# Taking the sign of float64 weights from GpSimd to ScalarE in a fused attention and bilinear MoE kernel

## The chip, the cores and the metric

The kernel runs on one core of one Trainium2 chip. The metric is the device time of one execution in microseconds; the figure compared is the median over several runs. The core has TensorE (PE in the profile), VectorE (DVE), ScalarE (ACT), GpSimd (POOL) and SyncE (SP), which here only issues DMAs.

## What is computed

The reference joins a pooled attention to a bilinear mixture layer. `q`, `k`, `v` have the shape (4, 8, 1152, 64); the weights come as float64 arrays.

```python
q_pool = q.reshape(B, H, S // 2, 2, D).mean(axis=3)          # 576 rows a head
scores = (1 / sqrt(D)) * q_pool @ k.T                         # 576 x 1152 a head
attn = exp(scores - max); attn = attn / (attn.sum() + 1e-9)
x = (attn @ v)  ->  (2304 tokens, 512)
out = ((x @ w_a) * (x @ w_b)) @ w_out                          # 512 -> 1536 -> 512
```

## The kernel before, in words

Work is cut into tasks. Each task is one small function of the kernel (`w_load`, `w_tail`, `w_sign`, `sm_max`, `moe_mm` and so on), registered by `add` with an engine, a planned cost and the names of the buffers that it reads and writes. `Plan.order` takes for each engine the sequence written out by hand in the table `ORDERS` (one list of task numbers for each of PE, DVE, ACT, POOL and SP) and merges the five lists; every engine then runs its own list strictly in order, and waits by semaphores where a buffer of another engine is not ready.

**Attention.** The 16 pairs of heads go by in passes; the first batch (pairs 0 to 3) goes in two rounds, the rest in one. A pass has blocks of 128 rows: TensorE makes the scores (`qk`, L768 or, split into halves of 16 bits, L770), VectorE reads them with a running minimum (`sm_max`, L800), ScalarE takes the exponential (`sm_exp`, L807), VectorE adds a constant and inverts the sum (`sm_sum` L811, `sm_rec` L817). From the second round on, ScalarE then writes the upper half of the probabilities in 16 bits (`sm_hi`, L820) and VectorE the rest (`sm_lo`, L824) into one of NPB buffers `p`; a DMA on the SP queue transposes the buffer into `pt` (L829), and TensorE multiplies by `v` (`pv`, L918). A buffer `p` may be written again when its transposition has landed. The four passes of the first round transpose on TensorE instead (L842) and use no `p`.

**Weights.** Behind the first four passes 36 tiles of 128 x 512 weights are prepared: f = 0 to 11 of `w_a`, `w_b` (m = 0, 1) and `w_out` (m = 2). A float64 arrives as two words of 32 bits in one of NRAW = 7 buffers `raw` (numbers 5 and 6 of them lie in `xt`). For each tile VectorE takes the largest magnitude of the upper words (`w_mag`, L596; then the short `w_real`, L602 and L604, `w_scale`, L646 and L650); ScalarE reduces the lower word to three bits (`w_tail`, L614); GpSimd reads the upper word as float32 and writes its sign as a 16-bit zero with a sign into the top of the lower word (`w_sign`, L618); ScalarE rescales the upper word in place (`w_z`, L609); VectorE shifts it left by three and joins the lower word to it by an OR (`w_join`, L624). The shift drops the sign bit of the upper word, so the sign comes from the lower word. Then ScalarE and GpSimd, or VectorE for `w_out`, split the float32 into two halves of 16 bits (`w_hi` L707, `w_lo` L712 or L714). The joined tile of `w_out` number f stands in the place of number f + 1 in `wo`, and one spare place at the end serves number 11.

**Bilinear layer.** Nine tiles of 256 tokens each run `moe_mm` (L999, TensorE), `moe_a` (L1034, ScalarE), `moe_g` (L1037, VectorE), the split `moe_gh` and `moe_gl` (L1042, L1045) and `moe_o` (L1064, TensorE), between the blocks of later passes; the last three tiles run after the last scores.

Of the kernel before, what the change touches and what calls it, by code (L numbers as in the profile page):

```python
# [92 lines left out]
    ),  # L93
    (
# [231 lines left out]
def kernel(  # L326
# [13 lines left out]
    def T(name, shape, dtype=F32):  # L340
        return sb.tile(shape, dtype, name=name)

    NS, NPB, NST, NG, NR = 3, 3, 12, 2, 6
    NRAW, NT_ = 7, 2 * B + 1
    wab = T("wab", [128, NF, 2, 2, KC, 128], F16)
    wo = T("wo", [128, NF + 1, 2, DM], F16)
# [56 lines left out]
    def ri(n):  # L403
        return n % NRAW
# [911 lines left out]
```

## Time and profile before

| | us |
|---|---|
| median of 3 runs | 824.94 |
| lowest and highest | 824.78, 828.25 |
| the profiled execution, its own time | 827.88 |
| span in its profile | 826.1 |
| TensorE busy in the span | 758.5 (92%) |
| VectorE busy | 647.6 (78%) |
| ScalarE busy | 570.8 (69%) |
| GpSimd busy | 228.8 (28%) |

Busy is time in which an engine works on an instruction, so an instruction that is held up in the middle counts as busy for its whole length. The shares are means over the whole span, and the load is not the same in all its stretches: it has to be looked at by stretches. A wait in the views stands for an engine that was idle, with the work that ended the idle time.

### The profile page before, as it was taken

How to read it: one execution, taken by the hardware profiler on the slowest of the kernel's cores; microseconds unless marked ns; L12 is line 12 of the kernel's file. 1: busy time of each engine (PE TensorE's matmuls, PEld its weight loads, DVE VectorE, ACT ScalarE, POOL GpSimd, SP SyncE). 2: the span in 40 equal slices, each digit the busy share in tenths (PEclk: the TensorE clock that was granted, in tenths of full speed). 3: DMA queues.
4: the chain of work that ended last, by engine and by line, in shares of the span. 5: the costliest groups of instructions: out<-in, count | busy, mean ns of one | idle time of the engine just before them, and what ended most of it. 6: DMA issues, size and time to landing. Idle time of an engine off the chain costs nothing. (4 is left out here: it accounts for less than half of the span.)

```text
span 826.1 us, 21393 instructions
## 1 busy us (share of the span) xinstructions
PE 758.5 (92%) x8906; PEld 564.5 (68%) x8906; DVE 647.6 (78%) x1283; ACT 570.8 (69%) x940; POOL 228.8 (28%) x206
## 2 busy tenths in 40 slices
PE   7787589988899988899999987999999999999998
PEld 5665367754677755687588645886687578677775
DVE  5989989999988888879979899898888984222222
ACT  5989879989777778768876887678767974321211
POOL 3879767943201122010402041103020320000000
PEclk9999689999999999999999999999999999999999
DMA  8275588999999999869979999879898976100100
GB/s 331 79 259 182 169 189 232 243 215 162 211 194 203 188 211 181 190 139 191 197 157 212 154 203 206 147 145 185 174 184 160 153 135 114 30 27 1 26 2 26
DMA packets 316433, 132.32 MB, mean 160 GB/s; under 512 B 300848, under 2 KB 302896, under 8 KB 316336
## 3 DMA queue, kind: packets, MB, share of 16 engines
q1 hardware_dynamic: 316336, 130.96, 76.0%
q8 instruction: 69, 1.13, 0.6%
q14 instruction: 28, 0.23, 0.1%
HBM read 50.72 MB, written 4.72 MB: 67 GB/s over the span
## 5 line engine op out<-in xcount | busy, mean ns | idle before, releaser
L999 PEld LDWEIGHTS <-wab 128*128 128x128 f16 x2592 | 251.3, 98 | 40.9 <-issue 4.5
L999 PE MATMUL ab<-xt,wab 128*128 128x256 f16 x2304 | 262.6, 273 | 3.6 <-DVE g L1037 2.4
L807 ACT ACTIVATE s<-s,st 128x1152 f32<-128x1152 f32 x144 | 179.7, 1248 | 23.3 <-DVE s L800 22.1
L824 DVE SCALAR_TENSOR_TENSOR p<-s,st,p 128x1152 f16<-128x1152 f32 x128 | 183.3, 1436 | 13.4 <-ACT p L820 12.5
L820 ACT ACTIVATE p<-s,st 128x1152 f16<-128x1152 f32 x128 | 159.5, 1249 | 48.3 <-DMA pt<-p 18.7
L1045 POOL TENSOR_TENSOR gl<-g,gh 128x256 f16<-128x256 f32 x72 | 60.1, 844 | 311.5 <-ACT gh L1042 195.8
L918 PE MATMUL xps<-pt,vs 128*64 128x128 f16 (+1 forms) x3888 | 109.1, 215 | 5.9 <-DMA pt<-p 3.4
L1037 DVE SCALAR_TENSOR_TENSOR g<-ab,cc,g 128x256 f32<-128x256 f32 x108 | 51.4, 479 | 80.5 <-ACT g L1034 79.8
L918 PEld LDWEIGHTS <-vs 128*64 128x64 f16 x3888 | 100.5, 111 | 18.6 <-issue 14.1
L1034 ACT ACTIVATE g<-ab 128x256 f32<-128x256 f32 x108 | 40.3, 376 | 101.4 <-PE ab L999 101.3
L800 DVE TENSOR_SCALAR_CACHE_REDUCE s<-sps,ksc 128x1152 f32<-128x1152 f32 x72 | 101.0, 1410 | 8.1 <-PE sps L770 7.5
L800 DVE TENSOR_SCALAR_CACHE_REDUCE s<-sps 128x1152 f32<-128x1152 f32 x72 | 96.3, 1349 | 13.2 <-PE sps L768 12.3
L768 PE MATMUL sps<-k,q 64*128 64x512 f32 (+2 forms) x480 | 93.8, 524 | 10.7 <-DVE s L800 9.4
L1064 PE MATMUL ab<-wo,gh 128*128 128x512 f16 x336 | 100.7, 380 | 2.4 <-DVE g L1037 1.0
L768 PEld LDWEIGHTS sps<-k,q 64*128 64x128 f32 (+1 forms) x480 | 61.2, 184 | 43.3 <-issue 21.2
L770 PE MATMUL sps<-k,q 64*128 64x512 f16 (+2 forms) x720 | 65.9, 324 | 6.8 <-DVE s L800 6.5
L1042 ACT ACTIVATE gh<-g 128x256 f16<-128x256 f32 x108 | 43.5, 407 | 38.4 <-PE ab L1064 20.0
L618 POOL TENSOR_SCALAR raw<-raw 128x512 f16<-128x512 f32 x26 | 62.0, 2385 | 22.9 <-ACT raw L614 8.4
L1064 PE MATMUL ab<-wo,gl 128*128 128x512 f16 x168 | 63.7, 379 | 3.8 <-POOL gl L1045 3.8
L1064 PEld LDWEIGHTS <-gh 128*128 128x128 f16 x432 | 39.0, 99 | 41.3 <-ACT gh L1042 1.5
L770 PEld LDWEIGHTS <-q 64*128 64x128 f16 (+1 forms) x720 | 40.3, 96 | 34.9 <-issue 15.2
L1064 PEld LDWEIGHTS <-gl 128*128 128x128 f16 x216 | 21.1, 98 | 33.1 <-POOL gl L1045 8.3
(135 smaller groups left out, 814.6 us busy)
## 6 DMA issues: line engine op xcount, KB each, us to landing
k<-in_k_dram SPq DMA_DIRECT2D x18, 576.0 KB, 5.2
vraw<-in_v_dram SPq DMA_DIRECT2D x17, 576.0 KB, 4.6
raw<-in_w_ab_dram SPq DMA_DIRECT2D x18, 512.0 KB, 4.7
qraw<-in_q_dram SPq DMA_DIRECT2D x12, 576.0 KB, 4.8
raw<-in_w_out_dram SPq DMA_DIRECT2D x8, 512.0 KB, 4.5
out_dram<-o SPq DMA_DIRECT2D x16, 256.0 KB, 2.6
xt<-in_w_ab_dram SPq DMA_DIRECT2D x6, 512.0 KB, 5.6
pt<-p SPq DMA_TRANSPOSE x128, 5.3
```

Source lines behind the costliest of these rows:

```text
L618: nc.gpsimd.tensor_scalar(out=raw_h[ri(n)], in0=raw_t[ri(n)][:, :, 1].bitcast(F32), scalar1=2.0 ** -100, scalar2=None, op0=ALU.mult)
L768: return nc.tensor.matmul(out, q, k, start=True, stop=True)
L770: return nc.tensor.matmul(out, q[:, hq], k[:, hk], start=(hq, hk) == (0, 0), stop=(hq, hk) == (1, 0))
L800: nc.vector.tensor_scalar(out=s_t[sbuf(i)], in0=sps[:, at:at + S], scalar1=-1.0 / 16.0 if u is None else ksc[:, u, 4:5], scalar2=None, op0 ...
L807: nc.scalar.activation(out=s, in_=s, func=AF.Exp, scale=-1.0, bias=t[:, 0:1], accum_out=t[:, 1:2])
L820: nc.scalar.activation(out=p_t[pbuf(i)][:, 0], in_=s_t[sbuf(i)], func=AF.Copy, scale=st_t[i % NST][:, 3:4])
L824: nc.vector.scalar_tensor_tensor(out=p[:, 1], in0=s, scalar=st_t[i % NST][:, 3:4], in1=p[:, 0], op0=ALU.mult, op1=ALU.subtract)
L918: nc.tensor.matmul(xps[half(e), at:at + w], vs[:, c, e, hv], pt[t][:, hp, c, c0:c0 + w], start=(c == 0 and n == 0), stop=(c == NCH - 1 and ...
L999: nc.tensor.matmul(dst if t < 8 else dst.rearrange("p (b n) -> p b n", b=B), wab[:, f, 1 - m, a, c], moe_x(t, b, c), start=(n == 0), stop= ...
L1037: nc.vector.scalar_tensor_tensor(out=g_t[:, f], in0=ab[j][:, 0], scalar=cc[:, t, f:f + 1], in1=g_t[:, f], op0=ALU.mult, op1=ALU.mult)
L1045: (nc.vector if dve else nc.gpsimd).tensor_tensor(out=gl_t[j], in0=g_t[:, f], in1=gh_t[j], op=ALU.subtract)
L1064: nc.tensor.matmul(out_bank(t, u), g[:, us], wo[:, f, a], start=(first and n == 0), stop=(last and n == 2))
```

## The change

`w_sign` goes. `w_z` becomes a parametric ReLU in place of a plain copy: for a negative weight the slope of -2^32 gives the magnitude times 2^32, and so sets a bit of the exponent that the later shift by three moves into the sign bit. One more buffer `p` is there (NPB from 3 to 4). `wo` loses its spare place; the last tile of `w_out` is joined in its `raw` buffer. Some planned costs are altered, and the order table is new: without `w_sign` every task keeps its engine, but tasks are renumbered and stand in another order (matched by name, 446 of 590 places in the list of TensorE hold another task than before, 879 of 1001 on VectorE, 670 of 762 on ScalarE, 165 of 241 on SP). On SP the loads begin q, k, k, w(1,0), w(1,1), v(1), w(2,0), v(0), q(1), k(1), where before they begin q, k, k, w(0,0), w(2,0), w(1,0), w(0,1), q(1), k(1).

```diff
 ORDERS = (
...
-    NS, NPB, NST, NG, NR = 3, 3, 12, 2, 6
+    NS, NPB, NST, NG, NR = 3, 4, 12, 2, 6
...
-    wo = T("wo", [128, NF + 1, 2, DM], F16)
+    wo = T("wo", [128, NF, 2, DM], F16)
...
-    raw_h = [x.rearrange("p n w -> p (n w)").bitcast(F16).rearrange("p (n h) -> p n h", h=4)[:, :, 1] for x in raw_t]
...
+    def in_place(f, m):
+        return m < 2 or f == NF - 1
+
     def zname(f, m):
-        return f"raw{ri(wn(f, m))}a" if m < 2 else f"w{f + 1}2"
+        return f"raw{ri(wn(f, m))}a" if in_place(f, m) else f"w{f + 1}2"
...
     def w_z(f, m, n):
         by = wz[:, 1, m, f:f + 1].bitcast(F32) if m < 2 else 2.0 ** -112
         up = raw_t[ri(n)][:, :, 1].bitcast(F32)
-        nc.scalar.activation(out=up, in_=up, func=AF.Copy, scale=by)
+        nc.scalar.activation(out=up, in_=up, func=AF.Prelu, scale=by, alpha=-(2.0 ** 32))
...
-    def w_sign(n):
-
-        nc.gpsimd.tensor_scalar(
-            out=raw_h[ri(n)], in0=raw_t[ri(n)][:, :, 1].bitcast(F32), scalar1=2.0 ** -100, scalar2=None,
-            op0=ALU.mult
-        )
...
         add("ACT", 0.555, key, w_tail, (n,), w=[rw + "l"])
-        add("POOL", 2.42, key, w_sign, (n,), r=[rw + "a"], w=[rw + "l"], port=False)
...
-        add("ACT", 0.6, key, w_z, (f, m, n), r=[f"wz{f}"] * (m < 2), w=[rw + "a"])
+        add("ACT", 0.65 if m < 2 else 0.56, key, w_z, (f, m, n), r=[f"wz{f}"] * (m < 2), w=[rw + "a"])
...
-        add("DVE", 0.32, key - 5, w_real, (0, 2, f, f + 1), r=mx, w=[x + "r" for x in mx], port=True)
+        add("DVE", 0.27, key - 5, w_real, (0, 2, f, f + 1), r=mx, w=[x + "r" for x in mx], port=True)
...
-        add("POOL", 0.04 * len(which) + 1.18 * n, key, x_lo, (p, j, which), r=xs + [x + "h" for x in names],
+        add("POOL", 0.33 + 0.3 * len(which), key, x_lo, (p, j, which), r=xs + [x + "h" for x in names],
```

## Rows read from the trace of the kernel before

**Rows 1.** The page, first part: span, then busy time by engine.

```profile
span 826.1 us, 21393 instructions
PE 758.5 (92%) x8906; PEld 564.5 (68%) x8906; DVE 647.6 (78%) x1283; ACT 570.8 (69%) x940; POOL 228.8 (28%) x206
```

**Rows 2.** Busy time by stretch: length, engines, TensorE clock, DMA share, GB/s.

```profile
0.00:20.65 20.65, 15.45 (x74) 10.69 (x76) 10.97 (x25) 10.74 (x18) 6.69 (x10) 1.00 0.90 331
20.65:206.50 185.85, 151.68 (x1591) 113.54 (x1587) 175.20 (x376) 164.10 (x291) 132.65 (x84) 0.94 0.75 192
206.50:702.00 495.50, 471.53 (x6236) 353.51 (x6237) 430.73 (x807) 368.09 (x562) 88.47 (x110) 1.00 0.94 176
702.00:826.10 124.10, 119.81 (x1011) 86.71 (x1008) 30.67 (x79) 27.83 (x71) 1.03 (x2) 1.00 0.07 19
```

**Rows 3.** The same view, one slice of the second stretch.

```profile
82.60:103.30 20.70, 10.65 (x68) 8.19 (x70) 20.36 (x43) 17.85 (x28) 15.15 (x11) 0.68 0.54 169
```

**Rows 4.** Groups of VectorE, 20.65 to 206.5 us: busy us, mean ns, idle before.

```profile
L824 DVE SCALAR_TENSOR_TENSOR p<-s,st,p 128x1152 f16<-128x1152 f32 x19 | 27.9, 1482 | 1.1 <-ACT p L820 1.1
L624 DVE SCALAR_TENSOR_TENSOR raw<-raw 128x512 int32<-128x512 int32 x18 | 14.6, 815 | 0.0
...
L714 DVE SCALAR_TENSOR_TENSOR wo<-wo,wr 128x512 f16<-128x512 f32 x11 | 9.4, 856 | 0.1
...
L602 DVE TENSOR_SCALAR wmx<-wmx 128x2 f32<-128x2 f32 (+1 forms) x11 | 5.7, 521 | 0.1
...
L604 DVE TENSOR_SCALAR wmx<-wmx 128x2 int32<-128x2 int32 (+1 forms) x11 | 4.7, 428 | 0.4
...
L650 DVE TENSOR_SCALAR wz<-wz 128x2 int32<-128x2 int32 x12 | 4.2, 354 | 0.4
```

**Rows 5.** Single lines of VectorE, 0 to 206.5 us: shortest, median, longest ns.

```profile
L602 DVE TENSOR_SCALAR wmx<-wmx x13: 151/284/1353, 15.2 to 167.5; 128x2 f32<-128x2 f32 x12, 128x12 f32<-128x12 f32 x1
L604 DVE TENSOR_SCALAR wmx<-wmx x13: 169/170/1306, 16.6 to 167.8; 128x2 int32<-128x2 int32 x12, 128x12 int32<-128x12 int32 x1
L650 DVE TENSOR_SCALAR wz<-wz x12: 169/237/974, 23.8 to 107.4; 128x2 int32<-128x2 int32 x12
L624 DVE SCALAR_TENSOR_TENSOR raw<-raw x18: 667/686/1621, 28.0 to 126.8; 128x512 int32<-128x512 int32 x18
L824 DVE SCALAR_TENSOR_TENSOR p<-s,st,p x19: 1398/1412/1816, 88.8 to 204.1; 128x1152 f16<-128x1152 f32 x19
L714 DVE SCALAR_TENSOR_TENSOR wo<-wo,wr x11: 727/743/1165, 173.7 to 203.4; 128x512 f16<-128x512 f32 x11
```

**Rows 6.** Instructions in order of time, 20 to 62 us: start, length.

```profile
20.85 6.96 POOL L618 TENSOR_SCALAR raw<-raw 128x512 f16<-128x512 f32 x3 [4.34 <-DMA xt<-in_w_ab_dram]
...
26.50 1.34 DVE L602 TENSOR_SCALAR wmx<-wmx 128x2 f32<-128x2 f32 x1
```

**Rows 7.** Groups of GpSimd, 20.65 to 206.5 us.

```profile
L618 POOL TENSOR_SCALAR raw<-raw 128x512 f16<-128x512 f32 x24 | 57.5, 2394 | 16.7 <-PE sps L768 7.7 <-DMA xt<-in_w_ab_dram 4.3 <-ACT raw L614 2.4
L618 POOL TENSOR_SCALAR xt<-xt 128x512 f16<-128x512 f32 x10 | 23.6, 2363 | 1.4 <-PE sps L768 0.6
```

**Rows 8.** Groups of ScalarE over the whole span.

```profile
L807 ACT ACTIVATE s<-s,st 128x1152 f32<-128x1152 f32 x144 | 179.7, 1248 | 23.3 <-DVE s L800 22.1
L820 ACT ACTIVATE p<-s,st 128x1152 f16<-128x1152 f32 x128 | 159.5, 1249 | 48.3 <-DMA pt<-p 18.7 <-DVE st L817 17.1 <-issue 5.2
...
L609 ACT ACTIVATE raw<-raw,wz 128x512 f32<-128x512 f32 x18 | 13.6, 770 | 1.4 <-POOL raw L618 0.8 <-DVE wz L650 0.6
...
L614 ACT ACT_TABLE_LOAD x1 | 1.3, 1283 | 0.7 <-PEq L1301 0.7
```

**Rows 9.** Waits, 206.5 to 702 us: us in total, times, longest.

```profile
ACT p L820 <- DMA pt<-p: 17.5, 15, 2.6
...
DVE p L824 <- ACT p L820: 11.4, 15, 1.4
...
PE sps L770 <- DVE s L800: 6.5, 5, 2.5
```

More of the change, by code (lines that the diff above doesn't have):

```diff
@@ L408, in wn @@
         return 2 * f + m if m < 2 else 2 * NF + f
+    def in_place(f, m):
+        return m < 2 or f == NF - 1
     def zname(f, m):
-        return f"raw{ri(wn(f, m))}a" if m < 2 else f"w{f + 1}2"
+        return f"raw{ri(wn(f, m))}a" if in_place(f, m) else f"w{f + 1}2"
     def zt(f, m):
-        return raw_t[ri(wn(f, m))][:, :, 1].bitcast(F32) if m < 2 else wo[:, f + 1].rearrange("p a n -> p (a n)").bitcast(F32)
+        return raw_t[ri(wn(f, m))][:, :, 1].bitcast(F32) if in_place(f, m) else wo[:, f + 1].rearrange("p a n -> p (a n)").bitcast(F32)
     ident, diag = g_t[:, 0, 0:128], [g_t[:, 1 + e, 0:128] for e in range(2)]
@@ L743, in prep_w @@
             on = LO_ON[m]
-            raw_last.append(add(on, 1.14 if on == "POOL" else 0.6, key, w_lo, (f, m), r=[z, f"w{f}{m}h"], w=[f"w{f}{m}l"], port=True))
+            raw_last.append(add(on, 1.18 if on == "POOL" else 0.6, key, w_lo, (f, m), r=[z, f"w{f}{m}h"], w=[f"w{f}{m}l"], port=True))
     def prep_wo(key):
```

291 rows, old and new, of the table ORDERS are left out of this document.

## The prediction

> **What bounds the kernel now.** I begin with the first part of the page [rows 1]: TensorE is busy for 92% of the span, VectorE for 78%. That mean hides two regimes, so the next view is busy time by stretch [rows 2]. From 20.65 to 206.5 us, while the weights are prepared behind the first passes, VectorE is busy 175.20 of 185.85 us (94.3%), ScalarE 164.10 (88.3%), and TensorE only 151.68, so VectorE sets the pace. From 206.5 to 702 us TensorE is busy 471.53 of 495.50 (95%), VectorE 430.73 (87%): TensorE sets the pace and loses 24.0 us. After 702 us TensorE alone has work (119.81 of 124.10). Nothing in the change shortens work of TensorE. So a gain has two places where it can come from: the second stretch, where VectorE must get shorter, and the 24.0 us that TensorE idles in the third.
>
> In the slice from 82.6 to 103.3 us VectorE is busy 20.36 of 20.70 us and TensorE 10.65, at a mean granted clock of 0.68 of 2.4 GHz [rows 3], so for a good part of the slice at the lower level, 1.2 GHz: TensorE waits for VectorE, and half its time there is idle.
>
> Then the groups of VectorE in the second stretch against the shortest and median lengths of the same lines [rows 4, 5]. `w_real` at L602 handles 2 numbers a partition. Its shortest is 151 ns, its mean 521, its longest 1353. The timeline shows why [rows 6]: one L602 starts at 26.50 us and runs for 1.34 us, to 27.84; three `w_sign` in a row on GpSimd run from 20.85 to 27.81. A short instruction of VectorE stood still until GpSimd was through. It counts as busy, so it hides in VectorE's 94.3%.
>
> **The change part by part.**
>
> *`w_sign` goes: VectorE.* How much of VectorE's time in the second stretch is such standing still? Count times (mean [rows 4] less undisturbed length, which I take as the median [rows 5], for L602 and L650 as 155 and 170, near their shortest): L602 11 x (521 - 155) = 4.0 us; L604 11 x (428 - 170) = 2.8; L650 12 x (354 - 170) = 2.2; the join L624 in `raw` 18 x (815 - 686) = 2.3; `sm_lo` L824 19 x (1482 - 1412) = 1.3; L714 11 x (856 - 743) = 1.2. That is 13.8 us. Nine further groups of this view are lengthened too, by 1.2 us at most each; I put them together at some 6.5, which makes 20.3 of VectorE's 175.20.
>
> GpSimd's other work (`w_lo`, `q_sum`, `moe_gl`, `x_lo`) stays, and it holds VectorE up as well. `w_sign` has 57.5 + 23.6 = 81.1 us of GpSimd's 132.65 in this stretch [rows 2, 7], 61%. Shared out by time, 0.61 x 20.3 = 12.4 us of VectorE's time goes. Lower bound 0.61 x 9.0 = 5.5 (the three short lines alone); upper bound 20.3 (if what is left of GpSimd's work no longer meets VectorE).
>
> *What of it reaches the end.* VectorE would come to 175.20 - 12.4 = 162.8 us, below the 164.10 of ScalarE. So ScalarE is late next. If ScalarE were then filled as VectorE is now, the stretch would take 164.10 / 0.943 = 174.0 us, a gain of 11.8. Two engines of equal load that hand blocks to each other fill worse than one that leads; at 90% the stretch takes 182.3 and gains 3.5. I take 9 (a filling of 92.8%). TensorE's 151.68 fit in 177 us, the more so as part of them ran at a lowered clock.
>
> *`w_sign` goes: latency.* A tile waits less between `w_tail` and `w_join`, and its buffer comes free sooner. ScalarE's `w_z` in `raw` waited for `w_sign` for only 0.8 us in all [rows 8], so I count nothing for it; the cover is the order of the lists, which had put other work in between.
>
> *`w_z` as parametric ReLU.* 36 instructions on ScalarE keep their size and place. The exponential and the plain copy of 128 x 1152 take 1248 and 1249 ns [rows 8], so the function does not show in the length there, and I leave each `w_z` at its present length (770 ns with its scale from a tile [rows 8]). Lower bound no gain, since the element count is the same. The upper bound is a reload of ScalarE's table at each change between exponential and ReLU; the trace has one load, of 1283 ns [rows 8]. Read by name, ScalarE's new list changes 46 times between `sm_exp` and `w_z`, so the bound is 46 x 1.283 = 59 us. I take nothing, as copy, square and exponential share one load in this trace, and keep 59 as a rival.
>
> The Trainium skill's page "ScalarE: Activation LUTs", section "Table sets: the hidden batching unit", puts cheap functions such as relu and copy into every set and prices a change of set, by its load with a drain, at about 2.66 us. It does not name the parametric ReLU. If that one is in no common set, an estimate by this page is 46 x 2.66 = 122 us on ScalarE; if it counts among the cheap ones, nothing. This trace agrees on the load itself (1283 ns) and shows no change of set.
>
> *A fourth buffer `p`.* `sm_hi` waited 17.5 us in 15 places for a transposition to land, and `sm_lo` 11.4 us in 15 places for `sm_hi`, in the third stretch [rows 9]. ScalarE and VectorE do not bind there; what counts is TensorE's wait for VectorE's reading of scores, 6.5 us in its largest row [rows 9] of 24.0 idle. Bounds: nothing (the stalls only fill ScalarE's idle time) and 11.4 (every wait of VectorE passes on to TensorE). I take 3.
>
> *The place in `wo`, the planned costs.* One join of 36 writes to another buffer, and that buffer is needed by no later load: nothing. Planned costs only merge the lists; each engine's own order is in the table: nothing.
>
> *The order table.* The same tasks stand otherwise. On SP the second pass's q and k are now behind three weight tiles and two loads of v (3 x 0.524 + 2 x 0.590 = 2.75 MB by their shapes) and not behind four weight tiles (2.10 MB): 0.65 MB at 331 GB/s [rows 2] is 2.0 us later. What waits there is SP's queue behind, and TensorE's scores of the second pass with VectorE's `sm_max` after them. VectorE is idle for half of the first 20.65 us and gets other work (magnitudes of v) sooner, so I take 1 us lost, bounds 0 and 2. `moe_a` of the first token tile comes one to two blocks of softmax earlier on ScalarE, which follows from weights that are ready sooner. For the rest of the table I take nothing; I cannot bound it from rows better than by 3 us either way.
>
> *The sum.* -9 - 3 + 1 = -11 us. On the profiled execution, 827.88 becomes 816.9. That execution is 2.94 above the median of the runs, so the median goes from 824.94 to 813.9; I predict 814.
>
> **The rivals.**
>
> *A. ScalarE takes over and the gain is mostly given back.* For it: 164.10 against 162.8 leave no lead. Against it: ScalarE has 21.75 us of idle in the stretch now, much of it waiting for VectorE's late results. At a filling of 90% or less, with nothing from the buffer and 2 us lost at the start, the gain is 3.5 - 2 = 1.5 or less: some 823.5.
>
> *B. More than forecast.* All 12.4 us reach the end as 11.8, the buffer brings 8 of its 11.4, and the start costs nothing: about 20 us, 805. For it: TensorE ran at a clock of 0.94 in that stretch, and a VectorE that is late less often keeps it nearer to 1. Against it: TensorE's idle time in the third stretch has several causes, and a buffer cures one.
>
> *C. Slower: table loads.* With 59 us more, ScalarE has 223 us of work in the stretch; at 94.3% it takes 236.6 us, 50.8 more than now. With the -3 and +1 of the other terms, 874. It decides from 9 loads on: 164.10 + 9 x 1.28 exceeds VectorE's present 175.20. For it: the trace shows no parametric ReLU. Against: three functions already live with one load.
>
> *D. Slower: the order.* A head of list that waits on SP for a load now placed later would stall each later DMA in that queue, transpositions too. 5 us, 830. Nothing in the rows points to one.
>
> **How the numbers follow.** Chances: the forecast (808 to 821) 0.58, A (mostly above 821) 0.17, B (below 808) 0.14, C 0.05, D 0.06. About 0.5%, 4.1 us, is what a measurement of this kernel can tell from no change. Faster than 820.8: the forecast, B and a quarter of A, 0.76. Within 4.1 us: the rest of A, 0.13, and 0.02 of D, so 0.15. Slower: 0.09. Range 804 to 823: it takes in A's middle and B's, and leaves out C, D and the far end of B.
>
> **What the next profile would show.** L618 gone, GpSimd's total down by some 86 us to about 143. L602, L604, L650 and L624 near their shortest lengths but for meetings with `w_lo`. VectorE's busy time in all down by 10 to 15 us, and TensorE's idle time in the first quarter down by about as much. `w_z` between 740 and 800 ns in `raw`, and one table load. ScalarE's wait for the transposition near nothing. The prediction is wrong if table loads appear, if the VectorE lines stay long (then GpSimd's other work held them), or if VectorE gets shorter and TensorE's busy share in the first quarter does not rise (rival A).

## The result, and the profile after

The median goes from 824.86 us (4 runs, 824.66 to 828.25) to 816.19 (4 runs, 813.69 to 817.30): a ratio of 0.9881 with a 95% interval of 0.9845 to 0.9917. That is 8.7 us between the medians and 9.8 by the ratio, which is of the means. The forecast was 814, 11 us less, with a range of 804 to 823. The same kernel on a second chip had 0.9840 (0.9814 to 0.9865).

The first part of the page after, for the execution of 817.21 us [rows 1]:

```profile
span 815.4 us, 21323 instructions
PE 762.5 (94%) x8906; PEld 571.1 (70%) x8906; DVE 638.1 (78%) x1283; ACT 568.1 (70%) x940; POOL 141.8 (17%) x170
```

GpSimd loses 87.0 us of its 228.8, of which `w_sign` was 85.6. VectorE loses 9.5 us with the same 1283 instructions: it does no less, it stands still less. TensorE's two numbers move against each other. Its idle time falls from 826.1 - 758.5 = 67.6 to 815.4 - 762.5 = 52.9 us, by 14.7, but its busy time grows by 4.0 with the same 8906 matmuls; 10.7 is left. By stretch [rows 2]:

```profile
0.00:20.65 20.65, 16.85 (x80) 12.41 (x81) 10.73 (x22) 11.61 (x21) 2.09 (x8) 1.00 0.89 334
20.65:206.50 185.85, 159.17 (x1600) 120.54 (x1600) 168.50 (x384) 165.60 (x293) 53.77 (x53) 0.90 0.79 198
206.50:702.00 495.50, 477.68 (x6440) 360.82 (x6439) 430.47 (x807) 364.68 (x562) 84.94 (x107) 1.00 0.93 175
702.00:815.40 113.40, 108.84 (x791) 77.30 (x789) 28.36 (x72) 26.19 (x67) 1.02 (x2) 1.00 0.05 15
```

In the second stretch VectorE (168.50 us) and ScalarE (165.60) are now almost equally loaded, at 91% and 89% of it, where VectorE led with 94% and 88% before. That is the pair of equals that rival A was built on. TensorE's mean granted clock there is 0.90, where it was 0.94: part of TensorE's longer busy time is time at 1.2 GHz instead of 2.4. This differs between executions of one kernel, so it cannot be laid to the change: in the profile of experiment 9, the same kernel in another execution, the clock of the second stretch is 0.94 as before, and TensorE is busy for 756.6 us, 1.9 less than before:

```profile
PE 756.6 (93%) x8906; PEld 565.2 (70%) x8906; DVE 636.8 (78%) x1283; ACT 567.7 (70%) x940; POOL 141.4 (17%) x170
20.65:206.50 185.85, 158.09 (x1669) 118.52 (x1669) 170.35 (x389) 166.91 (x296) 53.29 (x53) 0.94 0.82 200
```

The groups of VectorE in the second stretch that answer to [rows 4]:

```profile
L817 DVE SCALAR_TENSOR_TENSOR p<-s,st,p 128x1152 f16<-128x1152 f32 x20 | 28.1, 1410 | 0.2
L618 DVE SCALAR_TENSOR_TENSOR raw<-raw 128x512 int32<-128x512 int32 x19 | 14.0, 745 | 0.1
L708 DVE SCALAR_TENSOR_TENSOR wo<-wo,wr 128x512 f16<-128x512 f32 x11 | 8.6, 780 | 0.0
L603 DVE TENSOR_SCALAR wmx<-wmx 128x2 int32<-128x2 int32 (+1 forms) x13 | 3.5, 271 | 0.4
L644 DVE TENSOR_SCALAR wz<-wz 128x2 int32<-128x2 int32 x12 | 2.8, 236 | 0.4
L601 DVE TENSOR_SCALAR wmx<-wmx 128x2 f32<-128x2 f32 (+1 forms) x13 | 2.4, 181 | 0.1
...
L649 DVE TENSOR_SCALAR wsc<-wz 128x8 int32<-128x8 int32 x3 | 1.5, 486 | 0.0
```

The two numbers of `w_real` take 181 ns on the mean in place of 521, `sm_lo` is at its median of before. What is left above the shortest lengths (L603 at 271) is GpSimd's other work: the longest L603, 1105 ns, ends at 98.39 us, a `w_lo` of GpSimd beside it at 98.36. L649 shows that such meetings move about: 486 ns here against 254 before, three times.

ScalarE, with `w_z` at L610 [rows 8], and the waits of the third stretch [rows 9]:

```profile
L610 ACT ACTIVATE raw<-raw,wz 128x512 f32<-128x512 f32 x18 | 13.5, 770 | 0.7 <-DVE wz L644 0.7
...
L610 ACT ACTIVATE raw<-raw 128x512 f32<-128x512 f32 x8 | 5.6, 698 | 0.0
L610 ACT ACTIVATE xt<-xt,wz 128x512 f32<-128x512 f32 x6 | 4.6, 774 | 1.7 <-DVE wz L644 1.3 <-issue 0.4
...
L615 ACT ACT_TABLE_LOAD x1 | 1.3, 1283 | 0.7 <-PEq L1294 0.7
```

```profile
DVE p L817 <- ACT p L813: 16.4, 19, 2.3
...
PE sps L763 <- DVE s L793: 3.7, 3, 2.4
...
ACT p L813 <- DMA pt<-p: 3.2, 2, 1.7
```

The parametric ReLU takes the 770 ns of the copy, and one table load serves exponential, copy, square and it. The Trainium skill's page "ScalarE: Activation LUTs", section "Table sets: the hidden batching unit", leaves open whether this function is in the set of the exponential; this trace says that no further load is needed. ScalarE's wait for the transposition falls by 14.3 of its 17.5 us, while VectorE's wait for ScalarE grows from 11.4 to 16.4.

### The profile page after: what moved, and what is told of

Its sections match the earlier page's. It is cut to its first block, busy times and chain, and to the rows that moved or that the text cites. A ratio compares the mean times of both kernels' runs of the same rounds, so it can differ in the third digit from the quotient of the medians.

```text
span 815.4 us, 21323 instructions
## 1 busy us (share of the span) xinstructions
PE 762.5 (94%) x8906; PEld 571.1 (70%) x8906; DVE 638.1 (78%) x1283; ACT 568.1 (70%) x940; POOL 141.8 (17%) x170
## 4 chain that ended last, share of the span: by engine, by line
PE 41%; DVE 13%; issue 3%; ACT 3%; DMA 1%; SPq 0%; DVEq 0%; ACTq 0%
PE ab L992 19%; PE ab L1057 8%; PE sps L763 5%; PE xps L911 5%; DVE s L793 5%; DVE p L817 4%; PE sps L1057 3%; ACT p L813 1%; PE xps L1057 1%; DMA pt<-p 1%; DVE g L1030 1%; DMA k<-in_k_dram 1%; ACT s L800 1%; DVE vmx L521 1%; ACT k L471 0%
## 5 line engine op out<-in xcount | busy, mean ns | idle before, releaser
L817 DVE SCALAR_TENSOR_TENSOR p<-s,st,p 128x1152 f16<-128x1152 f32 x128 | 181.1, 1420 | 17.1 <-ACT p L813 16.4
L1038 POOL TENSOR_TENSOR gl<-g,gh 128x256 f16<-128x256 f32 x72 | 55.8, 784 | 224.3 <-ACT gh L1035 167.1
L763 PEld LDWEIGHTS <-q 64*128 64x128 f16 (+1 forms) x720 | 40.4, 97 | 31.4 <-issue 11.9
L1057 PEld LDWEIGHTS <-gl 128*128 128x128 f16 x216 | 21.1, 98 | 31.2 <-POOL gl L1038 6.5
L445 POOL TENSOR_TENSOR q<-qraw 128x576 f32<-128x576 f32 (+2 forms) x20 | 26.4, 1318 | 86.3 <-DMA qraw<-in_q_dram 30.5
```

The lines of the kernel that those rows point to most:

```text
L763: return nc.tensor.matmul(out, q[:, hq], k[:, hk], start=(hq, hk) == (0, 0), stop=(hq, hk) == (1, 0))
L817: nc.vector.scalar_tensor_tensor(out=p[:, 1], in0=s, scalar=st_t[i % NST][:, 3:4], in1=p[:, 0], op0=ALU.mult, op1=ALU.subtract)
L1038: (nc.vector if dve else nc.gpsimd).tensor_tensor(out=gl_t[j], in0=g_t[:, f], in1=gh_t[j], op=ALU.subtract)
L1057: nc.tensor.matmul(out_bank(t, u), g[:, us], wo[:, f, a], start=(first and n == 0), stop=(last and n == 2))
```

## The experiments

Three theories stood against each other. Theory 1 is that of the prediction: `w_sign` held VectorE up, and that is most of it. Theory 2: the new order table brings the gain. Theory 3: the fourth buffer does. Ratios are to the kernel before on the same chip, in interleaved runs.

**1. `w_sign` gone, old order, three buffers**

```diff
 ORDERS: the table of before without the 36 entries of w_sign
-    NS, NPB, NST, NG, NR = 3, 4, 12, 2, 6
+    NS, NPB, NST, NG, NR = 3, 3, 12, 2, 6
```

> The kernel after with the order table of before (the w_sign entries taken out of the list of GpSimd, nothing else moved) and three buffers p. Theory 1 (w_sign held VectorE up, and that alone is worth the larger part): 4 to 9 us below before, 816 to 821, with VectorE's busy time 8 to 12 us shorter. Theory 2 (the gain is the new order table's): within 2 us of before, VectorE's busy time shorter but idle in its place. Theory 3 (the gain is the fourth buffer's): within 2 us of before.

Ratio 0.9914 (0.9882 to 0.9945), 7.1 us of 827.47, with an interval of 4.6 to 9.8. The page and the groups of VectorE in its second stretch:

```profile
PE 764.3 (93%) x8906; PEld 569.8 (69%) x8906; DVE 638.9 (78%) x1283; ACT 569.1 (69%) x940; POOL 145.9 (18%) x170
```

```profile
L615 DVE SCALAR_TENSOR_TENSOR raw<-raw 128x512 int32<-128x512 int32 x18 | 12.7, 709 | 0.3 <-ACT raw L607 0.3
...
L641 DVE TENSOR_SCALAR wz<-wz 128x2 int32<-128x2 int32 x12 | 3.3, 273 | 0.4
...
L600 DVE TENSOR_SCALAR wmx<-wmx 128x2 int32<-128x2 int32 (+1 forms) x11 | 2.4, 215 | 0.4
L598 DVE TENSOR_SCALAR wmx<-wmx 128x2 f32<-128x2 f32 (+1 forms) x11 | 1.8, 161 | 0.1
```

VectorE is 8.7 us shorter than before, with the lists otherwise as they were, and most of the gain is there. Theories 2 and 3, which had this kernel within 2 us of before, fall as explanations of the larger part.

As the lists are otherwise the same, the traces also show where the gain is made. The reading of scores that ends at 203.5 us before ends here at 199.3:

```profile
202.16 1.33 DVE L800 TENSOR_SCALAR_CACHE_REDUCE s<-sps 128x1152 f32<-128x1152 f32 x1
```

```profile
198.01 1.33 DVE L790 TENSOR_SCALAR_CACHE_REDUCE s<-sps 128x1152 f32<-128x1152 f32 x1
```

It is 4.1 us earlier, as much as the two spans differ (826.1 and 822.0): between these two executions the whole gain is made by the end of the second stretch.

**2 and 12. The same with four buffers, twice**

```diff
 ORDERS: the table of before without the 36 entries of w_sign
```

> The kernel after with the order table of before (without the w_sign entries), four buffers p. Theory 1: the first experiment's time less 0 to 3 us. Theory 2: still within 2 us of before, some 9 us above the kernel after. Theory 3: 4 us or more below the first experiment, ScalarE's wait for the transposition near nothing.

> The second experiment's kernel once more (everything of the change but the order table), to tell the worth of the new table from the noise: the kernel after has had ratios of 0.988 and 0.984. If the table is worth nothing: 0.983 to 0.987 here. If it is worth 3 to 5 us: 0.988 to 0.992.

Ratios 0.9892 (0.9857 to 0.9928) and 0.9854 (0.9821 to 0.9887). These two hold all of the change but the table; the kernel after had 0.9881 and 0.9840. Taken together that is 0.9873 against 0.9861, about 1 us for the new table, with some 3 us either way from the four intervals; the single ratios, not all from one chip, spread by more. The new table by itself has no measurable worth over the old one.

**3. The kernel after with three buffers**

```diff
-    NS, NPB, NST, NG, NR = 3, 4, 12, 2, 6
+    NS, NPB, NST, NG, NR = 3, 3, 12, 2, 6
```

> The kernel after with three buffers p in place of four, all else as in it, the new order table too. Theory 1: 1 to 4 us above the kernel after (817 to 820). Theory 2: the new table was made for four buffers, so 2 to 6 us above. Theory 3: back near before, 822 or more.

Ratio 1.0283 (1.0241 to 1.0326): 852.37 us, some 36 above the kernel after. No theory had a loss of that size. Its waits over the span (in the kernel after the three are 3.2, 16.4 and 2.9 us):

```profile
ACT p L813 <- DMA pt<-p: 53.0, 25, 8.8
...
DVE p L817 <- ACT p L813: 33.5, 28, 4.2
...
PE ab L992 <- DVE g L1030: 19.9, 10, 6.7
```

The new lists place `sm_hi` as for four buffers. With three, ScalarE stands for 53.0 us at the head of its list until a transposition has landed; `moe_g` of VectorE stands behind, and TensorE waits 19.9 us for that. This chain is read from the waits; no run takes its links apart. With the old table, the same buffer is worth 2 us (experiment 8).

**4. The kernel after with `w_sign` back**

```diff
-        nc.scalar.activation(out=up, in_=up, func=AF.Prelu, scale=by, alpha=-(2.0 ** 32))
+        nc.scalar.activation(out=up, in_=up, func=AF.Copy, scale=by)
...
+        add("POOL", 2.42, key, w_sign, (n,), r=[rw + "a"], w=[rw + "l"], port=False)
```

> The kernel after with w_sign back on GpSimd and w_z a plain copy again; each w_sign stands in the new list of GpSimd where ScalarE's list has its w_tail or w_z, and 11 of the w_tail are moved ahead of their w_z on ScalarE. Four buffers, new table. Theory 1: 5 to 12 us above the kernel after, L602 and L604 with mean lengths of 400 ns and more again. Theory 2: within 3 us of the kernel after, since the table brings the gain. Theory 3: within 3 us of the kernel after.

Ratio 1.0449 (1.0407 to 1.0491): 865.37 us. Far more than theory 1 expected. Its mechanism is there, as VectorE is busy for 647.4 us again (638.1 in the kernel after), though the short lines, at 327 and 301 ns, stay below the 400 expected. But it is the smaller part. In the second stretch the waits lead:

```profile
ACT raw L611 <- POOL raw L620: 31.2, 12, 4.0
POOL raw L620 <- ACT raw L616: 18.6, 8, 3.4
```

The new lists put `w_z` close behind `w_tail`. With `w_sign` between the two, ScalarE waits 31.2 us for GpSimd. So 3 and 4 say little on what the buffer or `w_sign` is worth; they say that this table, written for one set of waits, does not carry another.

**5. The work of `w_sign` with nobody waiting for its result**

To part the two ways in which `w_sign` could cost (it holds VectorE up; `w_z` and `w_join` wait for it), experiment 1 gets 36 idle instructions of the same size at the old places.

```diff
+    def w_idle(n):
+        nc.gpsimd.tensor_scalar(
+            out=scratch[:, 0:512], in0=raw_t[ri(n)][:, 0:512, 0].bitcast(F32), scalar1=2.0 ** -100, scalar2=None, op0=ALU.mult
+        )
...
+        add("POOL", 2.42, key, w_idle, (n,), r=[rw + "l"], port=False)
```

> The first experiment's kernel (old order, parametric ReLU, three buffers p) with an idle GpSimd instruction of the size of w_sign at each of the 36 old places of w_sign: it reads the low words after w_tail and writes 512 numbers of 16 bits a partition into a scratch tile that nobody reads, so neither w_z nor w_join waits for it. Theory 1 (w_sign's price is that VectorE is held up while GpSimd works): back to before, ratio 0.997 to 1.003, VectorE's busy time 8 us or more above the first experiment's, L602's mean above 400 ns. Rival (its price is that w_z and w_join wait for it): as the first experiment, ratio 0.991.

Ratio 0.9997 (0.9971 to 1.0023): the whole of experiment 1's gain is gone. The page, VectorE's groups and GpSimd's new one:

```profile
PE 758.9 (92%) x8906; PEld 564.3 (68%) x8906; DVE 646.5 (78%) x1283; ACT 569.5 (69%) x940; POOL 227.6 (28%) x206
```

```profile
L625 DVE SCALAR_TENSOR_TENSOR raw<-raw 128x512 int32<-128x512 int32 x18 | 16.0, 896 | 0.0
...
L604 DVE TENSOR_SCALAR wmx<-wmx 128x2 int32<-128x2 int32 (+1 forms) x11 | 6.8, 619 | 0.4
...
L651 DVE TENSOR_SCALAR wz<-wz 128x2 int32<-128x2 int32 x12 | 6.3, 524 | 0.5
...
L602 DVE TENSOR_SCALAR wmx<-wmx 128x2 f32<-128x2 f32 (+1 forms) x11 | 3.2, 294 | 0.1
```

```profile
L620 POOL TENSOR_SCALAR scratch<-raw 128x512 f16<-128x512 f32 x26 | 60.1, 2313 | 25.5 <-PE sps L769 10.3 <-ACT raw L616 8.6 <-DMA xt<-in_w_ab_dram 4.4
```

Two of the signs named for theory 1 were not quite met: VectorE is 7.6 us busier than in experiment 1 and not 8, and L602 has 294 ns and not over 400; the standing still fell on L604 and L651 instead. Nobody reads what these instructions write, and yet the time is that of before. What stands behind them on GpSimd does not explain it: the waits of TensorE for GpSimd's work are no longer than in experiment 1 (`moe_o` for `moe_gl` 2.6 us against 3.8), and a load that reuses the buffer waited once, 0.4 us. So `w_sign` cost by being at work beside VectorE, and what waited for its result cost nothing that can be measured, within some 2 us. This is the experiment that settles the mechanism.

**6. The same work in quarters**

```diff
+        (four instructions of 128 columns in place of one of 512)
```

> As the experiment with idle GpSimd work, but each of its 36 instructions is cut into four of 128 columns, so GpSimd works at least as long in all. If VectorE waits for the end of the one GpSimd instruction that it meets, its lengthening falls by half or more, to 6 us or less of the 12.6, and the ratio lies between 0.991 and 0.996. If GpSimd's total working time is what slows VectorE, the ratio is that of the experiment with whole instructions.

Ratio 1.0274 (1.0235 to 1.0312), against an expected 0.991 to 0.996. The page, the groups, GpSimd's first quarter, and the second stretch:

```profile
PE 773.4 (91%) x8906; PEld 572.9 (67%) x8906; DVE 642.3 (75%) x1283; ACT 569.9 (67%) x940; POOL 267.9 (31%) x314
```

```profile
L604 DVE TENSOR_SCALAR wmx<-wmx 128x2 int32<-128x2 int32 (+1 forms) x11 | 4.0, 363 | 0.4
L660 DVE TENSOR_SCALAR wz<-wz 128x2 int32<-128x2 int32 x12 | 3.4, 281 | 0.4
...
L602 DVE TENSOR_SCALAR wmx<-wmx 128x2 f32<-128x2 f32 (+1 forms) x11 | 2.9, 261 | 0.1
```

```profile
L620 POOL TENSOR_SCALAR scratch<-raw 128x128 f16<-128x128 f32 x26 | 22.2, 853 | 14.4 <-ACT raw L616 6.3 <-PE sps L778 6.2
```

```profile
20.65:206.50 185.85, 141.58 (x1302) 107.46 (x1300) 146.59 (x337) 140.20 (x252) 160.08 (x177) 0.83 0.65 174
```

The mechanism came as expected: L604 falls from 619 ns to 363 and L651 (here L660) from 524 to 281, since VectorE waits for the end of a shorter instruction. VectorE's busy time is 3.4 us above that of experiment 1, where whole instructions had 7.6, although GpSimd works longer in all (267.9 us against 227.6): its total working time is not what slows VectorE. The Trainium skill's page "SBUF — State Buffer", section "Who interferes with whom", has GpSimd share a pair of ports with those instructions of VectorE that have two inputs in SBUF or use both of VectorE's ports, and the one that starts first keeps the pair for its whole length. The traces agree on the whole length for nearly all: of VectorE's instructions on two or four numbers that took over 400 ns, 17 of 19 in experiment 5 and all 7 in experiment 6 end 21 to 29 ns after an instruction of GpSimd; the other two were let go while it still ran. The time missed: a quarter takes 853 ns on the mean, not 2313 / 4 = 578, and GpSimd, busy 160.08 of 185.85 us, became the bound.

**7. The price of the parametric ReLU**

```diff
-        nc.scalar.activation(out=up, in_=up, func=AF.Prelu, scale=by, alpha=-(2.0 ** 32))
+        nc.scalar.activation(out=up, in_=up, func=AF.Copy, scale=by)
```

> The kernel after with w_z as a plain copy with a scale; the weights lose their sign, which nothing replaces. All theories: a parametric ReLU costs what a copy costs, so w_z has 770 and 676 ns (within 10) and the ratio to before is that of the kernel after, 0.988, within 0.003.

Ratio 0.9832 (0.9802 to 0.9862), which overlaps with both of the kernel after's, and lies 0.0049 below its first, outside the 0.003 expected, and 0.0008 below its second. The rows decide:

```profile
L610 ACT ACTIVATE raw<-raw,wz 128x512 f32<-128x512 f32 x18 | 13.5, 764 | 0.4 <-DVE wz L644 0.4
```

764 ns against 770: with the scale from a tile the function costs nothing over the copy. The eight in `raw` with a constant scale took 670 ns as a copy and 698 as a parametric ReLU, 0.2 us in all.

**8. The kernel before with a fourth buffer**

```diff
-    NS, NPB, NST, NG, NR = 3, 3, 12, 2, 6
+    NS, NPB, NST, NG, NR = 3, 4, 12, 2, 6
...
-        return f"raw{ri(wn(f, m))}a" if m < 2 else f"w{f + 1}2"
+        return f"raw{ri(wn(f, m))}a" if in_place(f, m) else f"w{f + 1}2"
```

> The kernel before with four buffers p and with the last tile of w_out joined in its raw buffer (the spare place in wo is gone, to make room); order table and w_sign as before. Theory 1: 0 to 3 us below before, ratio 0.996 to 1.000. Theory 3 (the fourth buffer is worth more): ratio below 0.995.

Ratio 0.9975 (0.9950 to 1.0000): about 2 us, at the edge of what can be told from nothing. Experiments 2 and 12 lie 0.0022 and 0.0060 below experiment 1, which agrees in sign. In the third stretch no wait of ScalarE for the transposition is left here (17.5 us before), and VectorE's wait for ScalarE is 11.6 us (11.4).

**9 to 11. Idle matmuls against TensorE's lowered clock**

In its first profile the kernel after has the lower clock for more of the time between 20.65 and 125 us than the kernel before. The two rows by stretch, before and after:

```profile
20.65:125.00 104.35, 78.65 (x735) 60.79 (x732) 96.17 (x230) 91.66 (x173) 81.66 (x50) 0.89 0.57 174
```

```profile
20.65:125.00 104.35, 81.98 (x692) 64.60 (x693) 89.44 (x234) 90.28 (x171) 32.68 (x30) 0.84 0.60 181
```

VectorE is 6.7 us less busy there, yet TensorE has fewer matmuls done (692 against 735) in more busy time. The attempt to give TensorE something to do in its waits:

```diff
+        if 0 < ps_.p < NP or ps_.again:
+            for _ in range(4):        # 8 in the other
+                nc.tensor.matmul(
+                    xps[:, 384:500], one.broadcast_to([128, 128]), one.broadcast_to([128, 116]), start=True, stop=True
+                )
         products = ((0, 0), (0, 1), (1, 0)) if ps_.split else (None,)
```

> The kernel after, unchanged, as the base for the two kernels beside it on the same chip: ratio 0.985 to 0.991.

> The kernel after with four idle matmuls of 128x116 ahead of the scores of each block of the first batch (passes over pairs 1 to 3 and the second round), into columns of PSUM that nobody reads, so that TensorE works while it waits for VectorE. If TensorE's lowered clock between 20 and 125 us takes back part of the gain: mean granted clock there above 0.95 (0.85 in the kernel after) and 2 to 5 us below it. If the lowered clock is hidden behind VectorE and ScalarE: within 1 us of it, or above it by the length of the idle matmuls that do not lie in waits, up to 10 us.

> As the kernel with four idle matmuls, with eight. If the lowered clock costs time: 2 to 6 us below the kernel after, the clock near 1. If it is hidden: above the one with four by its further idle matmuls, 2 to 10 us.

Ratios 0.9840 (0.9814 to 0.9865) for the kernel after, 0.9926 (0.9901 to 0.9951) with four, 1.0082 (1.0052 to 1.0112) with eight. The stretch and the idle matmuls of the one with four:

```profile
20.65:125.00 104.35, 85.74 (x750) 68.51 (x747) 82.47 (x225) 85.66 (x163) 31.86 (x30) 0.90 0.58 174
```

```profile
L772 PE MATMUL xps<-one 128*128 128x116 f32 x72 | 11.5, 308 | 1.0 <-DVE vsc L531 1.0
```

The clock is at 0.90, as in the unchanged kernel's own second profile (0.89), so the 0.84 that the attempt was made for was one execution's. The 72 matmuls of this stretch took 11.5 us of TensorE ahead of scores that VectorE needs; over the span TensorE is busy 16.4 us longer (773.0 against 756.6) and the median rises by 7.5 us (815.42 to 822.96), so a good part did not lie in the waits. With eight it rises by 11.9 more, past the 2 to 10 expected. So this neither cured the lowered clock nor tells what it costs; that stays open.

## Why the prediction was right, step by step

**VectorE is the bound of the second stretch, and part of its busy time is standing still beside `w_sign`.** Right, and shown from both sides: experiment 1 takes the work away and gains 7.1 us; experiment 5 puts it back with nobody waiting for its result and loses them all.

**12.4 us of VectorE's time.** As busy time this was too much: VectorE lost 9.5 us (8.7 in experiment 1). As a sum of lengths it was good. In the trace of before I count what instructions of VectorE up to 206.5 us take beyond the first quartile of their kind, where that is over 100 ns: it comes to 20.4 us, of which 12.4 lie beside `w_sign`; the prediction had 20.3 and 12.4. In the kernel after 7.2 us are left. What the step left out is that neighbours can be held up together, and busy time counts such a stretch once. Here `w_join` starts behind L604 and both stand until the `w_sign` beside them ends at 64.24 us:

```profile
61.96 2.28 POOL L618 TENSOR_SCALAR raw<-raw 128x512 f16<-128x512 f32 x1
...
62.96 1.31 DVE L604 TENSOR_SCALAR wmx<-wmx 128x2 int32<-128x2 int32 x1
63.04 1.23 DVE L624 SCALAR_TENSOR_TENSOR raw<-raw 128x512 int32<-128x512 int32 x1
```

Over the span the lengths of VectorE's instructions add up to 726.6 us before and 712.7 after, 14.0 less; 4.5 of that was overlap, and 9.5 is left.

**9 of it at the end, because ScalarE is next.** Measured 7.1, with an interval of 4.6 to 9.8 us (experiment 1), so 9 is not excluded. The two engines did come to equal loads, and the gain was made in this stretch (experiment 1). How it was worked out does not stand as well: ScalarE fills the stretch after to 89%, where the step took 92.8% and gave 3.5 us for 90%. The stretch has fixed ends and holds a little more work after than before, so its shares are not those of the step; with the 4.1 us of experiment 1's profile, ScalarE's 164.10 us would fill 181.75 to 90%. That 9 came near the measured gain, from a VectorE that lost 9.5 and not 12.4, is in part luck. The three signs of being wrong stayed away: there is one table load, VectorE's short lines are short, and TensorE's busy share in this stretch rose from 82% to 86%. But TensorE's idle time up to 206.5 us fell by 8.9 us, and VectorE's busy time by 9.5, both just under the 10 to 15 foreseen.

**Latency of `w_sign` at nothing, parametric ReLU at nothing.** Both right, as far as can be measured (experiments 5 and 7). Rival C is out: one table load, 770 ns.

**The fourth buffer at 3 us.** Right in sign, measured about 2, with an interval that touches nothing. ScalarE's wait went nearly whole, as forecast, but VectorE's wait for ScalarE did not fall: with the buffer alone it is 11.6 us against 11.4 (experiment 8), and its rise to 16.4 came with the new lists. What the step left out: the new lists need that buffer. Without it they lose 36 us.

**The order table at 1 us lost, for the start.** The start did not come later. The second pass's scores begin at 18.32 us, where the same ones began at 19.45; the larger bytes ahead of q and k were covered. Before, and then after:

```profile
19.45 2.21 PE L768 MATMUL sps<-k,q 64*128 64x512 f32 x12
```

```profile
6.05 0.65 SPq L440 DMA_DIRECT2D qraw<-in_q_dram  x1
...
6.75 0.72 SPq L434 DMA_DIRECT2D k<-in_k_dram  x1
...
18.32 2.21 PE L761 MATMUL sps<-k,q 64*128 64x512 f32 x12
```

As a whole the table is worth about 1 us of gain, with some 3 us either way (experiments 2 and 12 beside the kernel after). So the parts were 7.1 + 2 + 1 for 9 + 3 - 1. The errors of 1.9 and 1 us on the first two terms and of 2 us on this one have opposite signs, and that they left the sum 1.2 us from the 9.8 measured is luck; each of them is within the interval of its own measurement.

**The gain is not larger** (rival B), in part for the reason given there: TensorE's idle time after 206.5 us fell only from 28.3 to 22.4 us [rows 2]. The other part is the first term, 7.1 us in place of rival B's 11.8. That TensorE's clock stays nearer to 1 after the change is not excluded: over the runs beside experiments 9 to 11 its mean is 0.977 before (11 runs) and 0.982 after (6). What that brings was not taken apart.

## What to carry to other kernels

A busy engine can be standing still. Where a two-number instruction has a shortest length of 151 ns and a mean of 521, look for what runs on the neighbouring engine at that moment, and count the lengthening over all groups, but only once where neighbours are held up together; it was a better guide to the gain than any wait in the view of waits, which showed none of it. When a change comes with a new schedule, test the old schedule without the removed entries: here it had 7.1 us with three buffers and, with four, all of the gain as far as can be told, while each half-undone version of the new schedule was 36 to 49 us slower and would have misled about what the parts are worth.

## What the runs showed of the hardware that was not expected

Single lines of GpSimd in experiments 5 and 6, shortest, median and longest:

```profile
L620 POOL TENSOR_SCALAR scratch<-raw x26: 2214/2277/2750, 10.5 to 168.5; 128x512 f16<-128x512 f32 x26
```

```profile
L620 POOL TENSOR_SCALAR scratch<-raw x26: 709/719/1711, 11.1 to 195.0; 128x128 f16<-128x128 f32 x26
```

By the medians that is some 4.1 ns a column and a fixed 200 ns, so four quarters take about a quarter longer than the whole. The means (853 and 2313 ns) are longer, as GpSimd too takes longer beside long instructions of VectorE: the longest quarter, 1979 ns from 159.73 us, lies beside a `sm_lo` from 159.70 to 161.11 us. In all the 144 quarters took 123.3 us and the 36 whole ones 83.2, so cutting GpSimd's work to shorten its hold on VectorE cost GpSimd about half as much again.

In the kernel before, six of the 19 instructions of VectorE on two or four numbers that took over 400 ns ended while `w_sign` still ran, after 418 to 576 ns, and the other 13 ended 23 to 29 ns after an instruction of GpSimd. Why the six were let go sooner stays open.

Executions of one and the same kernel spread with TensorE's mean granted clock. Of the 11 runs of the kernel before beside experiments 9 to 11, the two with 0.985 and 0.986 took 825.26 and 826.72 us, the three with 0.971 took 829.08, 830.28 and 832.29. Which of the two is cause and which effect was not tried.
